# Seventeen small loads of 1 to 15, 64 and 32 partitions placed behind the last wo load of a decode kernel

## The chip, the cores and the metric

The kernel runs on one core of a Trainium2 chip. The core has five engines with instruction streams of their own: TensorE (PE in the profile; its weight loads are shown as PEld), VectorE (DVE), ScalarE (ACT), GpSimd (POOL) and SyncE (SP). They meet through semaphores. Sixteen DMA engines move data between the chip's main memory (HBM) and the core's on-chip memory (SBUF, 128 partitions). A DMA is issued by an instruction on SP, ACT or POOL, is spread over DMA engines, and raises a semaphore when it has landed; the kernel waits for a full count of 16.

The metric is the device time of one execution in microseconds, lower is better, as the median of several runs.

## What is computed

One token of a decoder layer: the input row is normalised, goes through attention over the last 4096 positions of a key and value cache (32 query heads, 4 key/value heads of 128) and, beside it, through a two-layer network with a GELU, and both results are added to the input.

```python
W = min(4096, max(256, Sk // 4))                       # 4096
x  = A_x                                               # [1, 1, 1024], bf16
xn = _layernorm(x)
# attention on xn
q = (xn @ wq).reshape(B, Sq, 32, 128).transpose(0, 2, 1, 3)
k = jnp.repeat(k_cache[:, :, Sk - W:, :], 8, axis=1)
v = jnp.repeat(v_cache[:, :, Sk - W:, :], 8, axis=1)
p = _softmax(jnp.einsum("bhqd,bhkd->bhqk", q, k) * 128 ** -0.5)
o = jnp.einsum("bhqk,bhkd->bhqd", p, v)
a = o.transpose(0, 2, 1, 3).reshape(B, Sq, 4096) @ wo  # wo is [4096, 1024]
# network on xn, with a layernorm of its own
h = _gelu(_layernorm(xn) @ w1 + b1)                    # w1 is [1024, 3584]
b = h @ w2 + b2                                        # w2 is [3584, 1024]
out = x + a + b
```

The weights and the used part of the cache are some 40 MB in bf16, read once for a single row of input.

## The kernel before

All large operands are loaded by SP, in the order in which SP's program has them: three chunks of wq into the tile WA (L179), the keys of heads 0 and 1 (L185), the two halves of w1 into the tile W1 (L195), the keys of heads 2 and 3, and the values of all four heads (L200), both into the tile KV, whose first half is named KT and whose second half V. Each load covers all 128 partitions with one contiguous row for each. None of them waits, since their tiles are free from the start.

Behind these SP waits until the matmuls with w1 are done (L419, count pe_h) and issues the two halves of w2 (L422) into the bytes of w1. Then it issues wo in seven chunks of 13, 9, 4, 2, 2, 1 and 1 of its 32 blocks of rows (L430), into the bytes of wq. A partition holds 32 rows of wo, and a chunk of one is 128 rows, one on every partition, 2 KB each. The last thing that SP does is to wait for DVE's copy of the second half of the result (L571), to issue its store (L572) and to wait for that (L574). ACT issues the three small loads of the input row and the biases at the start (L218 to L220), on a queue of its own, and the store of the first half of the result (L570).

TensorE's program is gathered in a list and written out at the end in three parts; every matmul has the line number 54 in the profile, so matmuls are told apart by their tiles. In order: the query projection from WA, scores of heads 0 and 1, the matmuls with w1, the scores of heads 2 and 3 (the last of these sets the count pe_sc, L426), the softmax's small matmuls, probabilities times values, w2, and at last wo, chunk by chunk as the chunks land (L554 to L562). The results of w2, wo, the bias and the input row add up in two rows of the accumulator memory, 512 columns each. When the last wo matmul is done, DVE copies one row (L566) and ACT the other (L568), and the two stores go out.

DVE transposes each head's keys in place in KT (L368) before the scores read them. After the last scores nothing reads KT again; V is read by the matmuls with the values.

Of the kernel before, what the change touches and what calls it, by code (L numbers as in the profile page):

```python
# [70 lines left out]
def bass_parallel_sum__sliding_block_cached__mixer_channel_mlp__decode_kernel(  # L71
# [21 lines left out]
    dve, act, pool, sp = nc.vector, nc.scalar, nc.gpsimd, nc.sync  # L93
# [13 lines left out]
    PE = Track(nc, "S_PE")  # L107
# [48 lines left out]
    KT = KV[:, 0:HKV * W]  # L156
# [269 lines left out]
    pe_sc = PE.mark(last)  # L426
# [33 lines left out]
    d_sump = DVE.mark(dve.tensor_reduce(out=SUMP[:, 0:1], in_=Pe[:, :], axis=AX.X, op=ALU.add))  # L460


    dve.wait_ge(PE.sem, pe_h)
    HH = PS[:, 2 * 512: 4 * 512].rearrange("p (n w) -> p n w", n=2)[:, :, 0:HW].rearrange(
        "p n (r c) -> p c n r", c=FC)
# [24 lines left out]
    for r in range(4):  # L490
        n = r // 2
# [80 lines left out]
    sp.dma_start(out_row[:, 512:1024], OUT[32:33, :]).then_inc(s_out[1], 16)  # L572
    act.wait_ge(s_out[0], 16)
    sp.wait_ge(s_out[1], 16)  # L574


    parts, at, size = [[]], 0, 0
    for op in pe.ops:
        n = 2 if op.name == "matmul" else 1
# [52 lines left out]
```

## Time and profile before

| | us |
|---|---|
| median of 7 runs | 100.44 |
| lowest and highest | 100.33, 100.89 |
| the profiled execution | 100.47 |
| its span | 99.06 |

The span runs from the first recorded instruction to the last landing; the rest of the profiled execution lies around it. One DMA engine's time is a sixteenth of the DMA share. Some of the transfers, as the page lists them by issue, with the size of each and the median time from issue to landing:

```profile
W<-in_B_w_dram SPq DMA_DIRECT2D x4, 3584.0 KB, 31.1
KV<-in_A_v_cache_dram SPq DMA_DIRECT2D x4, 1024.0 KB, 43.8
WA<-in_A_wo_dram SPq DMA_DIRECT2D x1, 3328.0 KB, 35.8
WA<-in_A_wo_dram SPq DMA_DIRECT2D x2, 256.0 KB, 42.1
```

Their long way to landing is time in the queue behind earlier loads. In the chain of waits, "SPq L430" is the time that SP's queue took to issue a wo chunk, and a piece "DMA WA<-in_A_wo_dram" is the time from an issue to the landing for which TensorE waited.

### The profile page before, as it was taken

The page shows a single profiled execution, that of the slowest core. Times are in us where ns is not written, and L with a number is a line of the kernel's source. Part 1 is how long each engine was busy: PE and PEld are TensorE (multiplying, and loading weights), DVE is VectorE, ACT ScalarE, POOL GpSimd, SP SyncE. Part 2 cuts the span into 40 slices and gives each one's busy share as a digit, 9 for nine tenths or more (in the row PEclk, how much of TensorE's full clock was granted, in tenths as well). Part 3 has the DMA queues.
Part 4 walks back from the last instruction along what each step waited for, and adds up shares of the span by engine and source line. Part 5 has one row for each costly group of instructions (what it writes and reads, how often), then busy time and mean ns, then how long its engine had stood idle before and what let it go on. Part 6 is the DMA issues. An engine that isn't in the chain of part 4 may idle for free.

```text
span 99.1 us, 826 instructions
## 1 busy us (share of the span) xinstructions
PE 51.3 (52%) x340; PEld 17.5 (18%) x340; DVE 35.9 (36%) x53; ACT 5.8 (6%) x11; POOL 4.6 (5%) x15
## 2 busy tenths in 40 slices
PE   0002475006700397907409555199964991696761
PEld 0002220002100132303003112033422330232110
DVE  4308520000289993000799743982025000000002
ACT  0500060000020000000000003100000000000002
POOL 6830000000000000000000000000000000000000
PEclk9999999999997559995885999556999999759999
DMA  5999899979998999989999999999998989999930
GB/s 195 473 389 465 374 423 490 476 334 427 526 397 370 475 428 394 475 349 430 433 420 423 423 490 394 509 394 394 486 417 369 495 376 451 417 395 412 400 119 1
DMA packets 3202, 39.89 MB, mean 403 GB/s; under 512 B 368, under 2 KB 384, under 8 KB 896
## 3 DMA queue, kind: packets, MB, share of 16 engines
q1 hardware_dynamic: 3170, 39.85, 95.1%
q8 instruction: 2, 0.03, 0.1%
q10 hardware_dynamic: 30, 0.01, 0.0%
HBM read 39.86 MB, written 0.00 MB: 402 GB/s over the span
## 4 chain that ended last, share of the span: by engine, by line
DMA 84%; SPq 9%; PE 4%; issue 1%; DVE 1%
DMA W<-in_B_w_dram 42%; DMA WA<-in_A_wo_dram 42%; SPq L430 6%; PE PS L54 4%; SPq L185 1%; SPq L422 1%; SPq L179 1%; DVE OUT L566 1%; SPq L195 0%
## 5 line engine op out<-in xcount | busy, mean ns | idle before, releaser
L368 DVE STREAM_TRANSPOSE KV<-KV 128x4096 bf16<-128x4096 bf16 x4 | 17.5, 4424 | 9.5 <-DMA KV<-in_A_k_cache_dram 9.5
L54 PE MATMUL PS<-KV,LQ 128*128 128x512 bf16 x32 | 10.6, 491 | 11.0 <-DVE KV L368 11.0
L54 PE MATMUL PS<-WA,OP 128*1 128x512 bf16 x64 | 9.7, 442 | 5.4 <-DMA WA<-in_A_wo_dram 5.3
L54 PE MATMUL PS<-WA,XNTb 128*1 128x512 bf16 x64 | 7.3, 623 | 7.5 <-DMA WA<-in_A_wq_dram 7.5
L54 PE MATMUL PS<-KV,PT 128*32 128x512 bf16 x32 | 9.0, 450 | 0.0
L566 DVE CAST OUT<-PS 1x512 bf16<-1x512 f32 x1 | 0.7, 684 | 21.0 <-PE PS L54 21.0
L54 PEld LDWEIGHTS PS<-KV,LQ 128*128 128x128 bf16 x32 | 3.5, 119 | 17.9 <-DVE KV L368 13.2
L54 PE MATMUL PS<-W,YTb 128*1 128x448 bf16 x64 | 4.7, 455 | 3.0 <-DMA W<-in_B_w_dram 3.0
L54 PE MATMUL PS<-W,GT 128*1 128x512 bf16 x56 | 6.2, 379 | 0.0
L340 DVE STREAM_TRANSPOSE TT<-PS 128x1024 f32<-128x1024 f32 x1 | 1.2, 1249 | 13.3 <-PE PS L54 13.3
L54 PEld LDWEIGHTS PS<-WA,OP 128*1 128x1 bf16 x64 | 2.8, 93 | 12.5 <-issue 5.8
L54 PE MATMUL PS<-XT,onesf 128*128 128x16 f32 x2 | 0.6, 383 | 8.3 <-DVE XT L287 8.3
L54 PEld LDWEIGHTS PS<-KV,PT 128*32 128x32 bf16 x32 | 3.5, 111 | 5.0 <-issue 2.5
L54 PEld LDWEIGHTS PS<-WA,XNTb 128*1 128x1 bf16 x64 | 1.7, 109 | 12.3 <-DMA WA<-in_A_wq_dram 9.4
L455 ACT ACTIVATE Pe<-PS,NMB 128x512 bf16<-128x512 f32 x2 | 1.3, 683 | 31.8 <-DVE NMB L452 31.8
L54 PEld LDWEIGHTS PS<-W,GT 128*1 128x1 bf16 x56 | 2.4, 84 | 3.4
L517 DVE TENSOR_TENSOR OHM<-PS,RM 32x512 f32<-32x512 f32 x1 | 0.7, 679 | 6.1 <-PE PS L54 6.1
L54 PEld LDWEIGHTS PS<-W,YTb 128*1 128x1 bf16 x64 | 1.6, 99 | 5.8 <-DMA W<-in_B_w_dram 3.4
L568 ACT ACTIVATE OUT<-PS 1x512 bf16<-1x512 f32 x1 | 0.6, 587 | 30.7 <-PE PS L54 30.7
L282 DVE STREAM_TRANSPOSE XTT<-XR 128x256 bf16<-128x256 bf16 x1 | 0.6, 625 | 4.0 <-DMA XR<-in_A_x_dram 4.0
L54 PEld LDWEIGHTS PS<-XT,onesf 128*128 128x128 f32 x2 | 0.5, 309 | 8.3 <-DVE XT L287 8.3
L434 DVE TENSOR_REDUCE MXP<-PS 128x1 f32<-128x1024 f32 x1 | 1.2, 1224 | 2.0 <-PE PS L54 2.0
(82 smaller groups left out, 28.4 us busy)
## 6 DMA issues: line engine op xcount, KB each, us to landing
W<-in_B_w_dram SPq DMA_DIRECT2D x4, 3584.0 KB, 31.1
WA<-in_A_wq_dram SPq DMA_DIRECT2D x1, 4096.0 KB, 21.9
KV<-in_A_k_cache_dram SPq DMA_DIRECT2D x4, 1024.0 KB, 34.9
KV<-in_A_v_cache_dram SPq DMA_DIRECT2D x4, 1024.0 KB, 43.8
WA<-in_A_wo_dram SPq DMA_DIRECT2D x1, 3328.0 KB, 35.8
WA<-in_A_wq_dram SPq DMA_DIRECT2D x1, 3072.0 KB, 12.5
WA<-in_A_wo_dram SPq DMA_DIRECT2D x1, 2304.0 KB, 40.9
WA<-in_A_wq_dram SPq DMA_DIRECT2D x1, 1024.0 KB, 6.1
```

What stands on the lines that cost most here:

```text
L54: ins = getattr(self.engine, op.name)(*op.args, **op.kwargs)
L179: sp.dma_start(WA[:, a:b], wq_pm[:, a:b]).then_inc(s_wq[j], 16)
L185: sp.dma_start(KT[:, g * W:(g + 1) * W], A_k_cache[0, g, SK - W:SK, :].rearrange("(m b) d -> m (b d)", m=128),).then_inc(s_k[g], 16)
L282: DVE.mark(dve.transpose(out=XTT[:, :].rearrange("p (k r) -> p k r", k=KC), in_=XR[:, :].rearrange("p (r k) -> p k r", k=KC)))
L340: DVE.mark(dve.transpose(out=TT[:, :], in_=PS[:, 0:1024]))
L368: d_k.append(DVE.mark(dve.transpose(out=KT[:, g * W:(g + 1) * W], in_=KT[:, g * W:(g + 1) * W])))
L422: sp.dma_start(W2[:, c0 * D:(c0 + nch) * D], w2_pm[:, c0 * D:(c0 + nch) * D]).then_inc(s_w2[j], 16)
L430: sp.dma_start(WA[:, j0 * D:(j0 + nj) * D], wo_pm[:, j0 * D:(j0 + nj) * D]).then_inc(s_wo[j], 16)
L434: d_mxp = DVE.mark(dve.tensor_reduce(out=MXP[:, 0:1], in_=PS[:, 4 * 512:6 * 512], axis=AX.X, op=ALU.max))
L455: a_exp = ACT.mark(act.activation(out=Pe[:, n * 512:(n + 1) * 512], in_=PS[:, (4 + n) * 512:(5 + n) * 512], func=ACTF.Exp, scale=SCALE, bi ...
L517: DVE.mark(dve.tensor_tensor(out=OHM[:, :].rearrange("p (g d) -> p g d", g=HKV), in0=PS[0:32, 0:512].rearrange("p (g d) -> p g d", g=HKV), ...
L566: d_out = DVE.mark(dve.tensor_copy(OUT[32:33, :], ACC[1]))
```

## The change

Behind the wo issues in SP's program it adds a wait for pe_sc and 17 loads from the first rows of wo: fifteen of n = 1 to 15 partitions, each with its own width of 32 + 4n elements (72 to 184 B for a row), one of 64 partitions with 1020 elements (2,040 B), and one of 32 partitions with 1012 elements (2,024 B). They are written to columns of KT that held the keys of head 1 and the first of head 2; no instruction reads them. All raise one new semaphore, s_tiny, by 16 each. At the end of its program SP waits for all of them, behind the wait for its store. The wo chunks stay as they were, every one of them on all 128 partitions.

```diff
@@ -460,6 +460,15 @@
     d_sump = DVE.mark(dve.tensor_reduce(out=SUMP[:, 0:1], in_=Pe[:, :], axis=AX.X, op=ALU.add))
 
 
+    s_tiny = nc.alloc_semaphore("s_tiny")
+    sp.wait_ge(PE.sem, pe_sc)
+    for n in range(1, 16):
+        w = 32 + 4 * n
+        sp.dma_start(KT[0:n, 4096 + n * 128: 4096 + n * 128 + w], A_wo[0:n, 0:w]).then_inc(s_tiny, 16)
+    sp.dma_start(KT[0:64, 6400:6400 + 1020], A_wo[0:64, 0:1020]).then_inc(s_tiny, 16)
+    sp.dma_start(KT[0:32, 7600:7600 + 1012], A_wo[0:32, 0:1012]).then_inc(s_tiny, 16)
+
+
     dve.wait_ge(PE.sem, pe_h)
@@ -572,6 +581,7 @@
     sp.dma_start(out_row[:, 512:1024], OUT[32:33, :]).then_inc(s_out[1], 16)
     act.wait_ge(s_out[0], 16)
     sp.wait_ge(s_out[1], 16)
+    sp.wait_ge(s_tiny, 17 * 16)
```

Every engine takes its own instructions in program order; the added lines stand between DVE's and are taken by SP alone, between the last wo issue and the wait before its store.

## The prediction

> **What bounds the kernel.** I read the busy times first, then the DMA queues, the chain of waits, the stretches at the end, and last the single packets of the trace. The whole 99.1 us is one stream of loads on SP's queue:
>
> ```profile
> span 99.1 us, 826 instructions
> PE 51.3 (52%) x340; PEld 17.5 (18%) x340; DVE 35.9 (36%) x53; ACT 5.8 (6%) x11; POOL 4.6 (5%) x15
> DMA packets 3202, 39.89 MB, mean 403 GB/s; under 512 B 368, under 2 KB 384, under 8 KB 896
> q1 hardware_dynamic: 3170, 39.85, 95.1%
> q8 instruction: 2, 0.03, 0.1%
> ```
>
> Queue q1 (SP's) fills 95.1% of all 16 DMA engines; no compute engine passes 52%. So only two things can move the end: a later landing of the last wo chunk, or something between that landing and the end. The chain of waits shows the second part in order of time (start, length, what):
>
> ```profile
> 50.45 0.51 SPq L430
> 50.95 0.04 issue
> 51.00 2.11 SPq L430
> 53.10 0.04 issue
> 53.15 2.13 SPq L430
> 55.27 0.04 issue
> 55.32 41.34 DMA WA<-in_A_wo_dram
> 96.66 0.04 issue
> 96.70 0.40 PE PS L54 x2
> 97.10 0.02 issue
> 97.12 0.68 DVE OUT L566
> ```
>
> The last wo chunk lands at 96.66, two matmuls and a 0.68 us cast follow, SP issues its half of the output at 97.84. Its data packet starts at 98.62 and the span ends at 99.06 when it lands. The profiled execution took 100.47 us, so 1.41 us lie around its span; the median is 100.44.
>
> The stretches at the end (length, busy time of PE, weight loads, DVE, ACT, POOL, clock, DMA share, GB/s) show where there is room:
>
> ```profile
> 88.00:94.00 6.00, 4.79 (x38) 1.40 (x34) 0.00 (x0) 0.00 (x0) 0.00 (x0) 0.93 0.97 394
> 94.00:95.00 1.00, 0.60 (x4) 0.09 (x4) 0.00 (x0) 0.00 (x0) 0.00 (x0) 1.00 0.74 275
> 95.00:96.70 1.70, 0.97 (x6) 0.17 (x6) 0.00 (x0) 0.00 (x0) 0.00 (x0) 1.00 0.09 35
> 96.70:99.06 2.36, 0.38 (x2) 0.08 (x2) 0.68 (x1) 0.59 (x1) 0.00 (x0) 1.00 0.00 1
> ```
>
> From 95.0 to 96.7 the DMA share is 0.09. That is two engines of 16 busy for 1.26 us: 2/16 x 1.26/1.70 = 0.093. The packets agree: on fourteen engines the last chunk's closing entry (its semaphore increment) starts by 94.97, on two at 96.25. From there until 98.6 the rings are empty.
>
> **The change part by part.** Nothing is removed. Added are a wait on SP, 17 issues, 17 loads, and a last wait.
>
> *The wait for the scores.* DVE's reduction behind the same count starts at 58.32, so it is met there. SP is busy issuing the last wo chunk until 59.00 (55.32 plus 3.68, the longest issue of L430). The wait costs nothing. Queued behind it on SP are the small issues and then the wait for DVE before L572, nothing else.
>
> *The issues.* SP has nothing to do from 59.00 to 97.84:
>
> ```profile
> SPq L572 <- DVE OUT L566: 38.8, 1, 38.8
> ```
>
> An unhindered issue took 0.43 us plus 0.04, so 17 x 0.47 = 8.0 us, done at 67.0. But the 2.11 above shows SP held back. A full-width load puts 8 data entries and one increment into each engine's ring. When a held issue ended, pushed minus started entries stood at 80.5 (21.22), 82.7 (23.36), 81 (53.11), 82.8 (55.28) and 80 (59.00); near the start it was 70 to 76. I take some 80 entries per engine as the room. How many does the change push? The page has 368 packets under 512 B: 22 loads x 16 increments = 352, and 8 + 4 + 2 + 1 + 1 for the loads of 8, 4 and 2 partitions and the two one-row stores. So a transfer of n partitions, n below 16, uses n engines, one row and one increment on each. I assume this to go on to 15, from the first engine up. The engine that is in all of them then gets 15 x 2 entries, 5 for the 64 partitions and 3 for the 32: 38. With 80 outstanding at 59.00, they are all accepted once 38 older ones have gone: the last two of V, 9 for each half of w2 and for two wo chunks, and some of the third, at 89.4, or 90.8 on a late engine. With room for 64 only, the second two-row chunk of wo would have to be reached, 93.8 at the latest. Both lie ahead of 97.84. Cost 0, cover 4.0 us at the least. Does a held SP slow the stream? In 5 to 24 us, when it was held for most of the time, the DMAs ran at 419 GB/s, in 24 to 48 us, free of it, at 429, in 48 to 60 us, held again, at 439: no.
>
> *The loads.* They are 17,600 B in the fifteen, 130,560 and 64,768 B in the two others: 0.213 MB, 0.5 us at 424 GB/s. On the fullest engine: 15 packets of 72 to 184 B, for which the nearest rows are 9 ns (88 B) and 27 ns (512 B), 6 packets of 2 KB at 84 ns, and 17 increments at 9 ns: 0.14 to 0.41 + 0.50 + 0.15 = 0.79 to 1.06 us. I take 0.9. It starts behind the engine's last wo packet: done at 95.9 if that engine is one of the fourteen, 97.2 if one of the two. The output packet wants it at 98.62, so 1.4 us are left in the worse case. The cover is the cast and the store's own way to the ring; without it the whole 0.9 us would show. No gain is possible here, since nothing leaves the stream. The two late engines aren't slowed by their neighbours: their 2 KB packets follow at 80 ns both while all run and while they are alone.
>
> The price of a tiny load behind another tiny one is not in the trace, only bounds. Below: 9 + 9 = 18 ns. Above: a load that must land before the next starts, 0.37 us (the one-row store, 98.51 to 98.885). The nearest rows are the last chunks, back to back in the same ring:
>
> ```profile
> 95.44 0.09 PEld L54 LDWEIGHTS PS<-WA,OP 128*1 128x1 bf16 x4 [1.17 <-DMA WA<-in_A_wo_dram]
> 96.06 0.08 PEld L54 LDWEIGHTS PS<-WA,OP 128*1 128x1 bf16 x2 [0.53 <-DMA WA<-in_A_wo_dram]
> 96.70 0.08 PEld L54 LDWEIGHTS PS<-WA,OP 128*1 128x1 bf16 x2 [0.56 <-DMA WA<-in_A_wo_dram]
> ```
>
> Two 256 KB chunks land 0.64 us apart, and 8 x 80 ns = 0.64: an increment makes no gap, though each lands 0.43 us after its entry starts. I take the low end.
>
> [...]
>
> *The last wait.* The small loads land by 97.2 + 0.43 = 97.7, ahead of 99.06. One more wait that is met: 0.04 us, the step between two SP pieces above.
>
> Sum: 0 + 0 + 0 + 0.04 on 100.47: **100.5 us**.
>
> **Rivals.**
>
> *A, the ring's tail:* each tiny load holds its ring until it has landed, and SP's output row stands behind them on the engine that has all. It decides from (98.62 - 96.26 - 0.65)/15 = 0.114 us for each on a late engine, (98.62 - 94.97 - 0.65)/15 = 0.20 on another. At 0.37 the ring is free at 96.26 + 0.65 + 5.55 = 102.5 or 101.2, the output later by 3.8 or 2.6: 104.3 or 103.1; at prices between, anything from 100.8 up. For it: no row shows two tiny loads back to back. Against: no gap at an increment, above. Slower.
>
> *B, SP held to the end:* if the room is counted in loads (9 or 10 outstanding at each held issue) rather than in entries, the tenth small load must wait for the last chunk at 96.70. Then 8 issues at 0.35 (the store's 0.31 plus 0.04) to 0.47 stand ahead of the output: 99.5 to 100.5 in place of 97.84, so 102.1 to 103.1. Against: the twelfth load's issue ended at 21.22 with no load landed since 13.4, though the eleventh's had ended at 16.37.
>
> *C, not behind:* the engines take the small loads in among the last chunks. Then 0.5 to 1.06 us come ahead of the last chunk: 101.0 to 101.5. Against: chunks of one queue have landed in the order of issue throughout.
>
> *D, the lag dealt anew:* two engines trail by 1.3 us from the start, and two 16,384 B instruction packets, 0.95 us each, ran at 4.18 and 9.69, just as they fell behind. A longer SP program could move or add such a fetch. On a late engine it adds up to 0.95 (101.4); if the lag went, up to 1.3 us would be gained (99.2). Against: both come early, the page has only these two, and SP's program with 23 + 17 DMAs stays shorter than DVE's with 53 busy instructions.
>
> **How the numbers follow.** Hidden 0.55, A 0.14, B 0.11, C 0.07, D 0.13 (0.08 faster, 0.05 slower). Within 0.3% (about what a measurement can tell from no change): 0.55; slower 0.14 + 0.11 + 0.07 + 0.05 = 0.37; faster 0.08. The hidden case alone spans 100.2 to 100.75. Up to 102.6 come C, the slow part of D, half of B and half of A: 0.55 + 0.07 + 0.05 + 0.055 + 0.07 = 0.80. Range 100.2 to 102.6.
>
> **What would show it.** In the profile after: SP's small issues end before 97.8 and its wait at L572's place is still put down to DVE; the last chunk lands near 96.7; the DMA share in 94 to 96.7 rises, that in the last microsecond doesn't; the output packet follows its issue by 0.8 us. I am wrong if that gap grows (A), if SP issues small loads after 96.7 (B), if the last chunk lands over 0.3 us later (C), or if the number or the place of the instruction packets changes (D).

## The result, and the profile after

The changed kernel takes 101.25 us in the median (100.75 to 101.49, 13 runs), the one before 100.44 (34 runs): a ratio of 1.0061, 95% interval 1.0046 to 1.0075. It is slower, by 0.6% as that ratio has it and by 0.8% between the two medians. The likeliest case of the forecast, that all is hidden, did not come; the time lies in the range stated.

The profiled execution took 100.65 us with a span of 99.2, 0.17 more than before. Its queues, from the page:

```profile
span 99.2 us, 843 instructions
DMA packets 3570, 40.11 MB, mean 404 GB/s; under 512 B 640, under 2 KB 752, under 8 KB 1264
q1 hardware_dynamic: 3538, 40.06, 96.1%
q8 instruction: 2, 0.03, 0.1%
```

843 - 826 = 17 instructions more, the loads. Packets under 512 B rose by 272: 120 tiny rows and 120 + 32 increments, so a load of n partitions did use n engines up to 15. The instruction packets are still two. What waited on SP's queue, and SP's issues (start, length):

```profile
SPq L581 <- DVE OUT L575: 9.0, 1, 9.0
```

```profile
48.94 10.07 SPq L430 DMA_DIRECT2D WA<-in_A_wo_dram  x7
59.98 27.69 SPq L467 DMA_DIRECT2D KV<-in_A_wo_dram  x15
87.71 0.56 SPq L468 DMA_DIRECT2D KV<-in_A_wo_dram  x1
88.32 0.71 SPq L469 DMA_DIRECT2D KV<-in_A_wo_dram  x1
98.01 0.24 SPq L581 DMA_DIRECT2D out_dram<-OUT  x1
```

The small issues end at 89.03; SP then still waits 9.0 us for DVE. The end of the chain of waits, and the stretches at the end (length, busy time by engine, clock, DMA share, GB/s):

```profile
55.32 41.51 DMA WA<-in_A_wo_dram
96.83 0.04 issue
96.88 0.40 PE PS L54 x2
97.27 0.03 issue
97.30 0.68 DVE OUT L575
```

```profile
94.00:95.00 1.00, 0.60 (x4) 0.09 (x4) 0.00 (x0) 0.00 (x0) 0.00 (x0) 1.00 1.14 366
95.00:96.70 1.70, 0.98 (x6) 0.17 (x6) 0.00 (x0) 0.00 (x0) 0.00 (x0) 1.00 0.52 108
96.70:99.20 2.50, 0.38 (x2) 0.08 (x2) 0.68 (x1) 0.59 (x1) 0.00 (x0) 0.94 0.02 7
```

From 95.0 to 96.7 the DMA share went from 0.09 to 0.52, as 0.2 MB more had to pass. The last wo chunk lands at 96.83 in place of 96.66, and everything behind it follows with the same distances: the whole 0.17 us is already there when the chunk lands.

This execution is one of the quicker ones. Each timed run has a span too, and those of the changed kernel, its first profile and the two later batches of it together, fall in two groups with nothing between: 99.2 to 99.5 (15 runs) and 99.8 to 100.3 (15 runs). Those of the kernel before lie between 98.9 and 99.3. So the change costs either about 0.3 or about 0.9 us from execution to execution, and the question is what decides.

(In some runs of either kernel the time around the span is 1.8 to 2.0 us in place of 1.4; the kernel before has a run with a span of 99.0 and a time of 100.83. It isn't the change's, and what it is stays open.)

The distinct widths help here. A late engine runs its small rows after its last wo row, so the widths that start last name the engines: the nth engine takes part in the loads of n or more partitions. Packets of the first profile from 96.25 us (start in us, bytes):

```
96.289 160   96.305 168   96.323 176   96.341 184        n = 12 .. 15: the 12th engine
             96.394 168   96.411 176   96.429 184        n = 13 .. 15: the 13th engine
```

### The profile page after: what moved, and what is told of

Its sections match the earlier page's. It is cut to its first block, busy times and chain, and to the rows that moved or that the text cites. A ratio compares the mean times of both kernels' runs of the same rounds, so it can differ in the third digit from the quotient of the medians.

```text
span 99.2 us, 843 instructions
## 1 busy us (share of the span) xinstructions
PE 54.3 (55%) x340; PEld 18.2 (18%) x340; DVE 35.9 (36%) x53; ACT 5.8 (6%) x11; POOL 4.6 (5%) x15
## 4 chain that ended last, share of the span: by engine, by line
DMA 84%; SPq 9%; PE 3%; issue 1%; DVE 1%
DMA W<-in_B_w_dram 42%; DMA WA<-in_A_wo_dram 42%; SPq L430 6%; PE PS L54 3%; SPq L185 1%; SPq L179 1%; SPq L422 1%; DVE OUT L575 1%; SPq L195 0%
## 5 line engine op out<-in xcount | busy, mean ns | idle before, releaser
L54 PE MATMUL PS<-KV,LQ 128*128 128x512 bf16 x32 | 12.7, 567 | 10.6 <-DVE KV L368 10.6
L54 PE MATMUL PS<-WA,OP 128*1 128x512 bf16 x64 | 8.1, 378 | 3.1 <-DMA WA<-in_A_wo_dram 3.1
L54 PE MATMUL PS<-KV,PT 128*32 128x512 bf16 x32 | 9.6, 473 | 0.0
L54 PE MATMUL PS<-W,GT 128*1 128x512 bf16 x56 | 7.9, 452 | 0.0
```

The costliest lines, as they stand in the source:

```text
L54: ins = getattr(self.engine, op.name)(*op.args, **op.kwargs)
```

## The experiments

In the diffs only the lines that differ from the changed kernel are shown. "Last chunk" is where the last wo chunk lands in the profile (before: 96.66).

**The changed kernel again** (e1_same; no edit).

> The changed kernel once more, for a second profile and as the base of the others on the same chip: about 101.2, +0.8 on the kernel before. Three theories for the 0.8. RING: the increments of the small loads pile up on the first engine's ring (17 of them) and SP's output row lands behind them. PATH: all 152 increments of the small loads go through one path that takes them at about 10 ns each, and the last wo chunk's own increments wait in it. BULK: the two loads of 64 and 32 partitions, 195 KB, write to SBUF beside the last wo chunk and hold it up. All three say +0.8 here; RING says that the gap from SP's store to its landing grows, PATH and BULK that the last chunk lands later.

Measured: 101.39 us, ratio 1.0074 (1.0047 to 1.0100). The profile fell in the slower group, 101.46 us with a span of 100.0:

```profile
55.18 42.39 DMA WA<-in_A_wo_dram
97.57 0.04 issue
97.61 0.40 PE PS L54 x2
98.01 0.02 issue
98.04 0.68 DVE OUT L575
```

```profile
59.92 27.89 SPq L467 DMA_DIRECT2D KV<-in_A_wo_dram  x15
87.86 0.56 SPq L468 DMA_DIRECT2D KV<-in_A_wo_dram  x1
88.46 0.71 SPq L469 DMA_DIRECT2D KV<-in_A_wo_dram  x1
98.75 0.24 SPq L581 DMA_DIRECT2D out_dram<-OUT  x1
```

The chunk lands at 97.57, 0.91 late; what follows it is as long as before. From SP's store to its landing it is 1.20 us here and in the first profile, against 1.19 before, so the output waits behind nothing: RING is out. The late engines here are the 6th and 7th. Their 2,048 B packets of wo from 95.0 us on last 154 ns in the mean and up to 258, where the kernel before has 85 in the mean and at most 91, and the first profile of the change, with the 12th and 13th late, 96 in the mean.

**Only the fifteen tiny loads** (e2_tiny15).

```diff
-    sp.dma_start(KT[0:64, 6400:6400 + 1020], A_wo[0:64, 0:1020]).then_inc(s_tiny, 16)
-    sp.dma_start(KT[0:32, 7600:7600 + 1012], A_wo[0:32, 0:1012]).then_inc(s_tiny, 16)
...
-    sp.wait_ge(s_tiny, 17 * 16)
+    sp.wait_ge(s_tiny, 15 * 16)
```

> Only the fifteen loads of 1 to 15 partitions, without the two of 64 and 32 partitions. RING: +0.7 (15 of 17 increments on the first engine stay). PATH: +0.6 (120 of 152 increments stay). BULK: 0 to +0.1.

Measured: 100.57 against 100.53 on the same chip, ratio 1.0006 (0.9997 to 1.0016), spans 99.0 to 99.3. The last chunk lands where it did:

```profile
55.26 41.37 DMA WA<-in_A_wo_dram
96.63 0.04 issue
96.67 0.40 PE PS L54 x2
```

The fifteen loads and their 120 increments cost nothing that shows. PATH falls with RING.

**Only the two wide loads** (e3_two).

```diff
-    for n in range(1, 16):
-        w = 32 + 4 * n
-        sp.dma_start(KT[0:n, 4096 + n * 128: 4096 + n * 128 + w], A_wo[0:n, 0:w]).then_inc(s_tiny, 16)
...
-    sp.wait_ge(s_tiny, 17 * 16)
+    sp.wait_ge(s_tiny, 2 * 16)
```

> Only the two loads of 64 and 32 partitions, without the fifteen. RING: 0 to +0.1 (2 increments on the first engine). PATH: +0.15 (32 increments). BULK: +0.8.

Measured: 101.31 us, ratio 1.0071 (1.0052 to 1.0091): the whole cost. BULK holds. The profile (last chunk 97.30, 0.64 late; span 99.7) has no widths that name its late engines.

**The fifteen with one partition each** (e4_one_row; the two wide loads stay).

```diff
-        sp.dma_start(KT[0:n, 4096 + n * 128: 4096 + n * 128 + w], A_wo[0:n, 0:w]).then_inc(s_tiny, 16)
+        sp.dma_start(KT[0:1, 4096 + n * 128: 4096 + n * 128 + w], A_wo[0:1, 0:w]).then_inc(s_tiny, 16)
```

> All 17 loads, but the fifteen small ones of one partition each, so that each uses the first engine alone. RING: +0.8 (still 17 increments on the first engine). PATH: +0.2 (15 + 32 = 47 increments). BULK: +0.8. If a load of one partition is spread over more engines than one, the landings show it, and the count of increments with it.

Measured: 100.96 us, ratio 1.0054 (1.0035 to 1.0073), spans 99.5 to 99.6 and 99.8 to 99.9. Each of these loads used a single engine: 15 + 32 = 47 increments land besides the 15 that are there at once (the first profile has 152, and 15 that come while SP issues, from 65.2 to 87.8 us). The profile's last chunk lands at 97.05, 0.39 late. The median lies between the numbers of the theories, because four of six runs fell in the quicker group; with two groups in every kernel that has the wide loads, a median says little, and the next experiments go by the profile and the spans.

**Why the wide loads are in the way of some engines.** A full-width load puts eight rows on each of the sixteen engines: on the two late ones before, each of the last two chunks is eight packets of 2,048 B and an increment. The loads of 64 and 32 partitions are spread over all sixteen engines as well (32 of the 152 new increments are theirs), but land in partitions 0 to 63 alone. And the loss went with the late pair: 0.17 us with the 12th and 13th, 0.91 with the 6th and 7th. From here on the author's guess, called PORT, is that wide loads to partitions 0 to 63 hold up a late pair of the first eight engines, and wide loads to 64 to 127 a late pair of the last eight. Why they should is not shown, nor which partitions an engine writes; what can be tried is which late pairs lose.

**The wide loads to the upper partitions** (e5_upper, and the same kernel again as e9_upper_again and e12_upper_third).

```diff
-    sp.dma_start(KT[0:64, 6400:6400 + 1020], A_wo[0:64, 0:1020]).then_inc(s_tiny, 16)
-    sp.dma_start(KT[0:32, 7600:7600 + 1012], A_wo[0:32, 0:1012]).then_inc(s_tiny, 16)
+    sp.dma_start(KT[64:128, 6400:6400 + 1020], A_wo[0:64, 0:1020]).then_inc(s_tiny, 16)
+    sp.dma_start(KT[64:96, 7600:7600 + 1012], A_wo[0:32, 0:1012]).then_inc(s_tiny, 16)
```

> The two loads to partitions 64 to 127 and 64 to 95 in place of 0 to 63 and 0 to 31. The widths in the profiles show which engines were the two late ones: the 12th and 13th in the first profile of the changed kernel (last chunk +0.15), the 6th and 7th in the second (+0.9). [...] Then the same mean here, +0.6 to +0.8, but with the halves changed: in the profile a late pair among the last eight loses 0.6 to 0.9, one among the first eight under 0.3. Rivals: SIZE (rows of 2,040 and 2,024 B are slow to write) and SOURCE (the rows lie side by side in HBM): +0.8, whichever engines are late.

Measured: 101.56 us, ratio 1.0114 (1.0080 to 1.0147): 1.06 us in the median, more than the 0.6 to 0.8 expected. The late engines of the profile are the 14th and 15th, and now engines of the last eight lose:

```profile
55.49 42.22 DMA WA<-in_A_wo_dram
97.71 0.04 issue
97.76 0.40 PE PS L54 x2
```

> The loads to partitions 64 and up once more, for a second profile of them. PORT: a late pair among the first eight engines loses under 0.35 at the last chunk (before: 96.66), one among the last eight 0.6 to 1.1 (the first profile had the 14th and 15th and lost 1.05). If a pair among the first eight loses as much as one among the last, PORT is wrong.

Measured: 102.05 us, ratio 1.0124 (1.0076 to 1.0171). This profile (100.89 us) has the 6th and 7th late, the pair that lost 0.91 with the loads below. Here it loses 0.36, a hundredth over the line that the expectation drew:

```profile
55.27 41.75 DMA WA<-in_A_wo_dram
97.02 0.04 issue
97.06 0.40 PE PS L54 x2
```

> The loads to partitions 64 and up a third time. Their times went up to 102.2, 0.6 more than PORT's 0.6 to 1.1 allow. If the profile falls on such a run, it tells whether the last chunk lands 1.6 later (more loss on the way in), or whether the time is lost behind it (the output, or the last wait for the small loads). On a run near 100.9 or 101.5 it adds a late pair to the table: among the last eight 0.6 or more, among the first eight 0.4 or less.

Measured: 101.77 us, ratio 1.0114 (1.0084 to 1.0144). The profile fell on a run of 101.95 us: late are the 12th and 13th, the pair that lost 0.17 with the loads below, the chunk lands at 97.68, and the span is 100.1. So the chunk does not land 1.6 late. The rest is time around the span, 1.85 us in place of 1.4, of the kind that the kernel before shows as well. Over the three batches the spans are 99.5 to 99.6 (2 runs) and 99.9 to 100.3 (12 runs); the higher ratios come from more runs in the slower group and from runs with the longer time around the span.

**The same bytes over all partitions** (e6_full).

```diff
-    sp.dma_start(KT[0:64, 6400:6400 + 1020], A_wo[0:64, 0:1020]).then_inc(s_tiny, 16)
-    sp.dma_start(KT[0:32, 7600:7600 + 1012], A_wo[0:32, 0:1012]).then_inc(s_tiny, 16)
+    sp.dma_start(KT[0:128, 6400:6400 + 510], A_wo[0:128, 0:510]).then_inc(s_tiny, 16)
+    sp.dma_start(KT[0:128, 7600:7600 + 253], A_wo[0:128, 0:253]).then_inc(s_tiny, 16)
```

> [...] SIZE: +0.8 or more, the rows are shorter still. SOURCE: +0.5 to +0.8, they lie in 256 KB in place of 128 KB.

Measured: 100.64 us against 100.50, ratio 1.0019 (1.0006 to 1.0033). All twelve spans lie between 99.1 and 99.4: the second group is gone. Last chunk 96.77, wo packets 88 ns:

```profile
55.32 41.46 DMA WA<-in_A_wo_dram
96.77 0.04 issue
96.82 0.40 PE PS L54 x2
```

**Rows of 2,048 B** (e7_size).

```diff
-    sp.dma_start(KT[0:64, 6400:6400 + 1020], A_wo[0:64, 0:1020]).then_inc(s_tiny, 16)
-    sp.dma_start(KT[0:32, 7600:7600 + 1012], A_wo[0:32, 0:1012]).then_inc(s_tiny, 16)
+    sp.dma_start(KT[0:64, 6400:6400 + 1024], A_wo[0:64, 0:1024]).then_inc(s_tiny, 16)
+    sp.dma_start(KT[0:32, 7600:7600 + 1024], A_wo[0:32, 0:1024]).then_inc(s_tiny, 16)
```

> The two loads with rows of 2,048 B, as the last chunks of wo have, in place of 2,040 and 2,024 B. PORT and SOURCE: +0.6 to +0.8 as before. SIZE: 0 to +0.1.

Measured: 100.93 us, ratio 1.0049 (1.0028 to 1.0070), spans 99.3 to 99.6 (8 runs) and 99.9 to 100.2 (3 runs), and one of 100.9 beyond both. The median is only 0.43 up, under the 0.6 to 0.8 of PORT and SOURCE, because most runs are of the quicker group. But both groups are there, so SIZE is out. The profile has the 14th and 15th late, with the chunk at 96.99.

**Source rows 64 KB apart** (e8_pitch).

```diff
-    sp.dma_start(KT[0:64, 6400:6400 + 1020], A_wo[0:64, 0:1020]).then_inc(s_tiny, 16)
-    sp.dma_start(KT[0:32, 7600:7600 + 1012], A_wo[0:32, 0:1012]).then_inc(s_tiny, 16)
+    sp.dma_start(KT[0:64, 6400:6400 + 1020], wo_pm[0:64, 0:1020]).then_inc(s_tiny, 16)
+    sp.dma_start(KT[0:32, 7600:7600 + 1012], wo_pm[0:32, 0:1012]).then_inc(s_tiny, 16)
```

> The two loads take their rows from HBM 64 KB apart, as the wo chunks do, in place of side by side; the destination stays. PORT and SIZE: +0.6 to +0.8. SOURCE: 0 to +0.1.

Measured: 100.86 us, ratio 1.0060 (1.0037 to 1.0082), spans 99.3 to 99.5 (5 runs) and 100.0 to 100.1 (4 runs). The profile, a run of 101.55 us, has the 6th and 7th late and loses 0.96:

```profile
55.31 42.31 DMA WA<-in_A_wo_dram
97.62 0.04 issue
97.67 0.40 PE PS L54 x2
```

The median is 0.36 up, again by the share of the groups; the slower group and this profile are what puts SOURCE out.

**The changed kernel a third time** (e10_same_again; no edit).

> The changed kernel a third time: a late pair among the first eight engines lands the last chunk at 97.5 or later, one among the last eight by 97.0. The median lies near 100.8 or near 101.4, by the share of each.

Measured: 101.31 us, ratio 1.0070 (1.0047 to 1.0093), runs at 100.73 to 100.86 and at 101.30 to 101.60. The profile has the 13th and 14th late and lands the chunk at 97.03, 0.03 over the line.

**The wide loads twice** (e11_double).

```diff
+    sp.dma_start(KT[0:64, 8700:8700 + 1020], A_wo[0:64, 0:1020]).then_inc(s_tiny, 16)
+    sp.dma_start(KT[0:32, 9800:9800 + 1012], A_wo[0:32, 0:1012]).then_inc(s_tiny, 16)
...
-    sp.wait_ge(s_tiny, 17 * 16)
+    sp.wait_ge(s_tiny, 19 * 16)
```

> The two loads twice (390 KB in place of 195 KB), to the lower partitions. [...] If what costs is the start of a load and not its bytes, all times grow by 0.1 at most.

Measured: 101.88 us, ratio 1.0140 (1.0098 to 1.0182), spans 100.0 (3 runs) and 100.4 to 101.3 (3 runs). In the profile the 7th and the 10th engine are late, one of the first eight and one of the last:

```profile
55.34 43.23 DMA WA<-in_A_wo_dram
98.57 0.04 issue
98.61 0.40 PE PS L54 x2
```

The chunk lands 1.91 late, twice the 0.91 and 0.96 of e1 and e8. The 7th engine starts its first small row at 97.50, the 10th at 96.80: side by side in one execution, the one of the first eight is 0.7 us behind the other. Not all of the 1.91 is in the rows. The 7th engine's last wo row ends at 97.49, 1.27 later than the last row in the kernel before (96.22); from there to the landing it takes 1.08 us in place of 0.44, and on the 10th engine 0.88. In e1 and e8 this last stretch is 0.58, in the first profile 0.44. Why it grows is not shown, and PORT says nothing of it.

The span is 2.27 longer, more than the chunk is late: the small loads' last increment lands at 101.28, 0.32 behind the output's at 100.96, so here the last wait costs time as well. The quicker group's loss grew to about 0.95, from some 0.3; how much of that is this wait isn't known.

Seen together:

| loads go to | late engines | last chunk | loss |
|---|---|---|---|
| (none, before) | not known | 96.66 | |
| lower half | 6th, 7th (e1) | 97.57 | 0.91 |
| lower half | 6th, 7th (e8) | 97.62 | 0.96 |
| lower half | 12th, 13th (first profile) | 96.83 | 0.17 |
| lower half | 13th, 14th (e10) | 97.03 | 0.37 |
| lower half | 14th, 15th (e7) | 96.99 | 0.33 |
| upper half | 14th, 15th (e5) | 97.71 | 1.05 |
| upper half | 12th, 13th (e12) | 97.68 | 1.02 |
| upper half | 6th, 7th (e9) | 97.02 | 0.36 |
| all partitions | 12th, 13th (e6) | 96.77 | 0.11 |

The same pairs, 6th with 7th, 12th with 13th, and 14th with 15th, lose up to 0.37 us or about 1 according to which half the wide loads write. That is what the runs show; what the rows of the wide loads and those of wo share on their way is not shown. The wo packets from 95.0 us on go the same way: in the mean 154 ns in e1, 144 in e8, 126 in e5 and 143 in e12, against 96 in the first profile, 101 in e10 and 109 in e9.

The losses of e3 and e4, 0.64 and 0.39, belong to engines that no width names, and e3's lies between the two sizes. So "up to 0.37" holds for the profiles of the table and not for every kernel here (more on this at the end).

Not tried: leaving out the last wait, since the small loads' increments could then land after the program's end (in e11 the last of them landed 0.32 us behind the output). No kernel here is faster than the one before.

## Why the prediction was right and wrong

The range held the time; the sum did not. That the range held is luck as far as the cause goes: it reached up to 102.6 for the sake of the rivals, and the delay came by none of their mechanisms. By its steps:

- *What bounds the kernel, and the two late engines:* right. In every profile the last chunk lands late on two engines, and it is this lateness on which the cost depends. In e1, e8 and e11 the small loads land behind the output besides, by 0.03, 0.08 and 0.32 us.
- *The issues:* right. The forecast had the last small issue at 89.4, or 90.8; it ended at 89.03, and DVE still is what SP waits for at L581. Rival B is out. The first issue started at 59.98 in place of 59.00, as the scores ended later in that execution; it cost nothing.
- *The tiny loads:* right in the sum. One tiny row with its increment follows another at 17 ns (120 B at 94.608, 128 B at 94.625), against 18 ns taken, and the fifteen cost 0.04 us with an interval about none. Something like rival A's mechanism exists: eleven packets of 2,040 B behind the tiny ones lasted 341 to 952 ns in the first profile, two over 300 where one engine has all the tiny loads (e4), none over 209 in the kernel without them (e3). That they wait for tiny loads to land is argued, not shown. But it holds engines that are done with wo, and the output's way stayed at 1.20 us.
- *The last wait:* mis-sized. The small loads were to land by 97.7; the last of them did at 98.69, 1.74 us behind the last entry, 0.5 us ahead of the output. In e1 it landed at 99.98, 0.03 behind the output. It costs next to nothing, but its cover is gone there. The term took 0.43 us from the last entry to its landing, as for one load; the increments of one engine land 0.18 to 0.20 us apart, though their entries start 17 ns apart. So it depends on how many small loads a late engine has: the 6th engine, late in e1, has 12, the first has 17. Five more at 0.20 would put the end about 1 us behind the output, an estimate; no profile has a late engine before the 6th.
- *The step that failed* is the sentence "The two late engines aren't slowed by their neighbours: their 2 KB packets follow at 80 ns both while all run and while they are alone." The rows were right, but in both stretches every load in the rings was one to all 128 partitions. The wide loads put rows of all sixteen engines into half of the partitions, and beside them the late engines of e1 had their packets at 154 ns in place of 85. The step cost the bytes by each engine's own ring, 0.9 us behind its own last wo packet; they had to be costed by where they land, too. The runs show that the loss goes with the half; by what mechanism is not shown. The term that stood at 0 measured 0.17 to 0.37 us in one group and 0.91 to 0.96 in the other.
- *Rival C* had the sign and nearly the size, 101.0 to 101.5, with the last chunk over 0.3 us late as its mark. Its mechanism did not come: the small rows ran behind wo on every engine. *Rival D* did not come either; there are two instruction packets as before.

Open is the smaller part, the 0.17 to 0.37 us that late engines of the other eight lose. The same bytes over all partitions cost 0.11 in the profile, so some of it goes with any traffic beside a late engine, and with the bytes doubled the 10th engine's part of the chunk landed at 97.68, 1.02 later than the last chunk of the kernel before. Where that comes from was not tried.

## What to carry to other kernels

Work that is queued behind a critical load is behind it only on each engine's own ring: engines that finish early start it while the late ones are still in the critical load (here the DMA share from 95.0 to 96.7 us went from 0.09 to 0.52). Cost it by where it writes as well as by which queue it is in, and spread it over all partitions: the same 195 KB cost 0.14 us over 128 partitions, and some 0.3 or 0.9, from execution to execution, over 64 and 32. A wait for many small loads at the end has a cost of its own: count the increments on one engine, 0.18 to 0.20 us each here. Where times fall in two groups, look for what differs between executions (here which two engines are late) before a mean is explained.

## What the runs showed that was not expected

- The late engines change from execution to execution: 6th and 7th, 7th and 10th, 11th and 12th (e2), 12th and 13th, 13th and 14th, 14th and 15th were seen; in the kernel before two trail by 1.3 us. In every profile two instruction packets of 16,384 B, 0.88 to 0.98 us long, ran near 4 and 10 us. That they make the two engines late was argued, not tried, but their lengths speak for it, since they go with the late pair: 0.88 to 0.89 us each with the 6th and 7th (e1, e8, e9), 0.92 to 0.93 and 0.96 to 0.97 with the 12th and 13th (first profile, e6, e12), 0.97 and 0.96 with the 13th and 14th (e10), 0.97 to 0.98 and 0.95 with the 14th and 15th (e5, e7). By that, an inference, e3 (0.97 and 0.96) had two of the 13th to 15th late and e4 (0.93 and 0.97) the 12th and 13th, engines of the last eight. Then these lost 0.64 without the tiny loads and 0.39 with them on one engine, in place of 0.17 to 0.37, and their loss is not always the small one.
- Increments can trail far behind their entries: 1.74 us in the first profile, against 0.4 us for a full-width load. In e4, where one engine has all the tiny loads, they land 0.18 to 0.20 us apart; the last eight distances in e11 are 0.20; where two engines are late they alternate, at 76 to 105 ns for the last six in the first profile.
- SP's queue took issues until about 80 entries for each engine were outstanding (80 to 82.8 when a held issue ended, before), and by this count the end of the 17 issues came out within 0.4 us of the earlier of the two figures (89.4).
- The packet times in the prediction stand 0.04 us late against the page's zero; those behind it are on the page's.
